# Second expert product turned round: w2 stationary, outputs as [d, token], and expert 0 on blocks of 512 tokens

## The chip, the cores and the metric

The kernel runs on one core of one Trainium2 chip. The metric is device time in microseconds of one execution, the median over the runs shown. TensorE does the matrix products (its matmul rows are called PE in the profile and its weight loads PEld), VectorE is DVE, ScalarE is ACT, GpSimd is POOL, and SyncE (SP) issues transfers.

## The reference, cut to what matters

Three parts follow each other. A delta-rule recurrence over 768 tokens of 4 batches and 8 heads gives x of 3072 x 384. A mixture of 8 experts, all of them on all tokens, is gated by P, which eight Sinkhorn iterations make from the logits of all tokens. A second network follows.

```
for t in range(768):                                   # per batch and head, 48 x 48 state
    y[t]  = q[t] @ state
    state = state + beta[t] * outer(k_n[t], v[t] - k_n[t] @ state)
x = y as [3072, 384]
P = sinkhorn(exp(x @ w_gate))                          # [3072, 8], 8 iterations over all tokens
for e in range(8):
    out += P[:, e:e+1] * (maximum(x @ w1[e], 0) @ w2[e])   # 384 -> 1024 -> 384
h = out @ w_in                                         # 384 -> 2048
result = (h * cos(h)) @ w_out                          # 2048 -> 384
```

## The kernel before, in words

**Products.** Every fp32 product is three TensorE passes over a head and a tail of each operand: head by head, head by tail, tail by head. `h_mms` (L112) makes 128 hidden columns f of a first product for a block of tokens: 9 matmuls (3 slices of d, 3 passes), w1 stationary, the tokens moving. `relu_split` (L134) takes them out of the PSUM bank: ACT writes the head, DVE the tail. `y_mms` (L125) makes the second product of 128 tokens: 3 matmuls with h stationary and 384 columns of w2 moving, so the result is [token, d]. In TensorE's rows L119 is a first product and L129 a second one.

**Attention.** The recurrence runs in 24 units of 128 tokens (chunks of 32 tokens of the 4 batches). `SEQ` (L29) spells, letter by letter, what TensorE does in a tick (one unit's time): K and k are the products of state with keys and queries (L311, L324), U, S and P the in-chunk solve, the state update and the output (L348, L362, L379), X the transposes of x (L397), G and g the gate's logits (L417, L431), T and B the transposes and the Gram products of a unit to come (L231, L249), N the operations of its normalisation on DVE and ACT (L191), W a weight split (L104), w filler matmuls (L558). Each m is half a step of expert 0 (`half`, L643): either one first product (`moe0_h`, L488) or one second product (`moe0_y`, L496). Between the letters `inv_some` (L547) issues operations of a triangular inversion on POOL (`inv_ops`, L275, rows L291 and L297); it must be done at every fourth tick, ahead of K. Until the first m, `fill` (L164) puts filler matmuls between the pieces of small matmuls.

```
29  SEQ = (..., "KXmNWmUmTGmkSmmNPgBmm", "KWmkmUXmTgBmSmPmTBNmm", "KmXkUTmNmSmmGPmmgBm")
638 mq.append((2 * ((s + 1) // FT) + 2, lambda s=s: moe0_h(s + 1)))
```

**Expert 0 before** goes over blocks of 256 tokens, as soon as two units are done (L635 to L639): eight m a tick from tick 2 on. A first product is 9 matmuls of 256 columns into one of two banks `hb`; a second product is 6 matmuls of 384 columns into `yb[0:2]`. Its output is written, not yet gated, to DRAM (`ysc`). What is left of expert 0 after the last tick runs at L715, with a Sinkhorn piece (`sk_some`, L481) at every fourth half; the remaining pieces run one a step in expert 1 (L921). `load_kq` and the weight loads of expert 0 go by SP's queue.

**Experts 1 to 7** are 336 steps of 512 tokens and 128 hidden columns (L777; 7 experts, 6 blocks, 8 slices f). A step of TensorE is `moe_h` of the next step (9 matmuls of 512 columns) and `moe_y` of this one (12 matmuls of 384 columns into the four banks `ybk`). After a block's eighth step DVE adds the four banks, each times its gate, to `acc` (L797; the gate is one scalar for each partition, a partition being a token). Weights come in groups of two slices f: `w_load` (L94) loads them into staging tiles by POOL's queue, `w_split` (L104) writes head and tail.

**The second network** wants its input as [d, token], so `x2_T` (L806) transposes `acc` on TensorE, three transposes for 128 tokens, and ACT and DVE split them. `net_step` and `net_y` (L873) work in three banks `hb2` (L827) and four `ybk`; the cosine's chain runs on ACT, POOL and DVE.

Of the kernel before, what the change touches and what calls it, by code (L numbers as in the profile page):

```python
# [34 lines left out]
def kernel(  # L35
# [28 lines left out]
    stg = ctx.enter_context(tc.tile_pool(name="stg", bufs=1))  # L64
# [7 lines left out]
    ysc = [dram.tile([128, 4, DM], F32, name=f"ysc{b}") for b in range(NB)]  # L72
# [6 lines left out]
    beta_sb = const.tile([128, S // C, C], F32, name="beta_sb")  # L79
# [11 lines left out]
    NG = FT // 2  # L91
    w1_t, w2_t, st1_t, st2_t = {}, {}, {}, {}

    def w_load(n):  # L94
        st1 = stg.tile([128, KD, 256], F32, tag="st1", name="st1")
        st2 = stg.tile([128, 2, DM], F32, tag="st2", name="st2")
        e, g = divmod(n, NG)
        a, b = w1[e, :, g * 256:(g + 1) * 256], w2[e, g * 256:(g + 1) * 256, :]
        q_ = nc.sync if n < NG else nc.gpsimd
        q_.dma_start(out=st1, in_=a.rearrange("(k p) f -> p k f", p=128))  # L100
        q_.dma_start(out=st2, in_=b.rearrange("(j p) d -> p j d", p=128))
        st1_t[n], st2_t[n] = st1, st2
# [30 lines left out]

    def relu_split(h, ps, nn):  # L134
# [861 lines left out]
```

## Time and profile before

| what | us |
|---|---|
| median of 3 runs | 2340.44 |
| lowest and highest run | 2336.85, 2342.12 |
| span of the profiled execution | 2340.3 |
| PE busy in it | 2266.8 (97%) |
| DVE busy | 1040.9 (44%) |
| ACT busy | 641.3 (27%) |
| POOL busy | 345.9 (15%) |

The span is the time of the one execution that the profiler recorded, from its first to its last instruction, and it stands beside the median within 0.2 us. Busy shares are means over stages that differ: the attention units end near 487 us, the rest of expert 0 near 510, experts 1 to 7 near 1926, and the second network fills the rest. "Granted clock" is TensorE's clock as a share of its full speed.

### The profile page before, as it was taken

To read this page: it belongs to the slowest core of one execution; us is meant where nothing else is said; L and a number is where in the kernel's file an instruction comes from. 1 tells how busy PE (TensorE), PEld (TensorE's weight loads), DVE (VectorE), ACT (ScalarE), POOL (GpSimd) and SP (SyncE) were. 2 spreads that over 40 slices of the span, in tenths; PEclk is the share of its full clock that TensorE was granted. 3 is DMA by queue.
4 is the path that set the end of the run, shared out by engine and by line. 5 is a ranking of instruction groups with operands and counts; after the bars stand their busy time and mean duration, and the time that the engine had idled before them with its cause. 6 is when DMAs were issued, how large, how long until landed. Compare 5 with 4: busy or idle time off the path is not lost.

```text
span 2340.3 us, 46677 instructions
## 1 busy us (share of the span) xinstructions
PE 2266.8 (97%) x20327; PEld 2027.2 (87%) x20327; DVE 1040.9 (44%) x2109; ACT 641.3 (27%) x1169; POOL 345.9 (15%) x599
## 2 busy tenths in 40 slices
PE   5889999999999999999999999999999999999998
PEld 3578888889999999999999999999999989888897
DVE  8455554345244324333333433433332226666665
ACT  1222222232122112112111211211111126566665
POOL 6256654210000000000000100000000011111111
PEclk7799999999999999999999999999999999999999
DMA  4233222153012002101100200110010130000000
GB/s 76 72 87 72 67 68 58 54 204 142 14 48 62 17 24 68 41 17 55 51 28 18 78 28 28 58 38 28 7 55 28 54 108 1 14 14 14 14 14 14
DMA packets 132221, 113.23 MB, mean 48 GB/s; under 512 B 80880, under 2 KB 121008, under 8 KB 131248
## 3 DMA queue, kind: packets, MB, share of 16 engines
q1 hardware_dynamic: 121936, 64.63, 10.2%
q0 software_dynamic: 10080, 45.62, 5.8%
q8 instruction: 159, 2.61, 0.4%
q14 instruction: 46, 0.38, 0.1%
HBM read 78.75 MB, written 31.46 MB: 47 GB/s over the span
## 4 chain that ended last, share of the span: by engine, by line
PE 89%; DVE 4%; POOL 4%; issue 2%; ACT 1%; DMA 1%; SPq 1%; POOLq 0%; ACTq 0%; DVEq 0%
PE hb L119 39%; PE yb L129 22%; PE pa L129 19%; PE pa L119 3%; POOL Xsys L297 1%; PE pa L341 1%; POOL tmp L291 1%; PE pa L354 1%; PE pa L385 1%; PE yb L167 1%; PE pa L238 1%; DVE Bst L304 1%; PE pa L257 0%; DVE S L374 0%; SPq L177 0%
## 5 line engine op out<-in xcount | busy, mean ns | idle before, releaser
L119 PE MATMUL hb<-x,w1t 128*128 128x512 f32 x3366 | 840.1, 394 | 0.0
L119 PEld LDWEIGHTS hb<-x,w1t 128*128 128x128 f32 x3366 | 624.9, 188 | 113.6
L136 DVE SCALAR_TENSOR_TENSOR h<-hb,h 128x512 fp32r<-128x512 f32 (+1 forms) x432 | 273.1, 632 | 964.2 <-ACT h L135 964.0
L129 PE MATMUL yb<-w2t,h 128*128 128x384 f32 x2952 | 605.6, 340 | 3.4 <-ACT tp L846 1.8
L135 ACT ACTIVATE h<-hb 128x512 fp32r<-128x512 f32 (+1 forms) x432 | 238.1, 551 | 1293.1 <-PE hb L119 1289.2
L129 PEld LDWEIGHTS yb<-w2t,h 128*128 128x128 f32 x2952 | 524.5, 188 | 42.1 <-ACT acc L882 3.1
L129 PE MATMUL pa<-w2t,h 128*128 128x384 f32 x2376 | 475.6, 334 | 0.0
L129 PEld LDWEIGHTS pa<-w2t,h 128*128 128x128 f32 x2376 | 420.7, 188 | 0.1
L100 POOL DMA_DIRECT2D st<-in_moe_w_dram x28 | 21.5, 769 | 1221.2 <-DVE w1t L109 1221.2
L119 PE MATMUL hb<-xb,w1t 128*128 128x256 f32 x864 | 130.0, 296 | 5.8 <-DVE xb L407 4.3
L119 PEld LDWEIGHTS hb<-xb,w1t 128*128 128x128 f32 x864 | 112.3, 194 | 11.3 <-DVE xb L407 4.7
L847 POOL TENSOR_SCALAR tp<-tp 128x512 f32<-128x512 f32 x96 | 60.1, 626 | 332.6 <-ACT tp L846 332.5
L297 POOL TENSOR_TENSOR Xsys<-Xsys,tmp 128x30 f32<-128x30 f32 (+9 forms) x150 | 80.5, 536 | 11.8
L866 ACT ACTIVATE h<-tp 128x512 fp32r<-128x512 f32 x96 | 60.7, 632 | 74.2 <-DVE tp L861 69.2
L855 ACT ACTIVATE tp<-tp 128x512 f32<-128x512 f32 x96 | 60.7, 632 | 68.1 <-DVE tp L852 68.1
L861 DVE TENSOR_TENSOR tp<-tp,hb 128x512 f32<-128x512 f32 x61 | 41.9, 688 | 80.1 <-ACT tp L860 80.1
L291 POOL TENSOR_TENSOR tmp<-Nsys,Xsys 128x30 f32<-128x30 f32 (+9 forms) x150 | 75.6, 504 | 11.2
L860 ACT ACTIVATE tp<-tp,small 128x512 f32<-128x512 f32 x96 | 68.7, 715 | 0.0
L871 DVE TENSOR_TENSOR h<-tp,h 128x512 fp32r<-128x512 f32 x96 | 65.6, 683 | 0.8 <-ACT h L866 0.8
L341 PEld LDWEIGHTS pa<-S,KT 48*32 48x32 f32 x2944 | 33.2, 107 | 21.8 <-DVE D L321 8.7
L119 PE MATMUL hb<-x 128*128 128x512 f32 x207 | 51.7, 394 | 0.0
L341 PE MATMUL pa<-S,KT 48*32 48x48 f32 x2944 | 42.8, 215 | 8.8 <-DVE D L321 6.3
(168 smaller groups left out, 1790.3 us busy)
## 6 DMA issues: line engine op xcount, KB each, us to landing
st<-in_moe_w_dram POOLq DMA_DIRECT2D x56, 384.0 KB, 4.0
xsc<-xb SPq DMA_DIRECT2D x24, 384.0 KB, 3.2
x<-xsc POOLq DMA_DIRECT2D x6, 1536.0 KB, 9.9
tp<-in_moe_w_in_dram SPq DMA_DIRECT2D x16, 384.0 KB, 3.5
wsa<-tp SPq DMA_DIRECT2D x32, 192.0 KB, 2.0
tp<-in_moe_w_out_dram SPq DMA_DIRECT2D x16, 384.0 KB, 3.3
wsb<-tp SPq DMA_DIRECT2D x32, 192.0 KB, 1.9
kr<-in_k_dram SPq DMA_DIRECT2D x96, 48.0 KB, 2.3
```

Source lines behind the costliest of these rows:

```text
L119: nc.tensor.matmul(out=ps[:, :nn], lhsT=w[:, a, kk, fs], rhs=x[:, b, kk, c0:c0 + nn], start=(i == 0), stop=(i == 3 * KD - 1),)
L129: nc.tensor.matmul(out=ps[:, :DM], lhsT=h[:, a, ts], rhs=w[:, b, f % 2, :], start=(first and i == 0), stop=(last and i == 2),)
L135: nc.scalar.activation(out=h[:, 0, :nn], in_=ps[:, :nn], func=ACTF.Relu)
L136: nc.vector.scalar_tensor_tensor(out=h[:, 1, :nn], in0=ps[:, :nn], scalar=0.0, in1=h[:, 0, :nn].bitcast(F32), op0=ALU.max, op1=ALU.subtract,)
L291: e.tensor_tensor(out=a, in0=Nsys[:, j + 1:, j:j + 1].to_broadcast([128, n, c1 - c0]), in1=Xsys[:, j:j + 1, c0:c1].to_broadcast([128, n, c ...
L297: e.tensor_tensor(out=x, in0=x, in1=a, op=ALU.subtract)
L341: nc.tensor.matmul(out=pa[i][b * C:(b + 1) * C, kq * 192 + j * D:kq * 192 + (j + 1) * D], lhsT=kt[r0:r0 + D, kq, j, b * C:(b + 1) * C], rh ...
L847: nc.gpsimd.tensor_scalar(out=a, in0=a, scalar1=-MAGIC, scalar2=1.0, op0=ALU.add, op1=ALU.mult)
L855: nc.scalar.activation(out=rr[i % 2], in_=rr[i % 2], func=ACTF.Abs)
L860: nc.scalar.activation(out=c, in_=rr[i % 2], func=ACTF.Sin, scale=-1.0, bias=half_pi)
L866: nc.scalar.activation(out=h[:, 0], in_=c, func=ACTF.Copy)
L871: nc.vector.tensor_tensor(out=h[:, 1], in0=cc[i % 2], in1=h[:, 0].bitcast(F32), op=ALU.subtract)
```

## The change

What it does:

- `yT_mms` takes the place of `y_mms` in all experts: w2 is the stationary side and h the moving one, 9 matmuls of 512 columns into three banks, one for each 128 rows of d; the result is [d, token].
- Expert 0 goes over blocks of 512 tokens with four units done ahead, four m a tick from tick 4 on instead of eight from tick 2; a first product has the one bank `hb`, a second one three banks `yb`. The gate's logits are made for 512 tokens at once, every fourth tick.
- Experts 1 to 7 alternate by block between the banks `pa[0:3]` and `yb`, and by step between `hb` and `pa[3]` once the Sinkhorn pieces are done.
- The gate now varies along the free axis: `sk_T` transposes P and writes it to DRAM; `p_load` loads a block's gate row, broadcast over the partitions, by SP's queue; `moe_acc` multiplies on DVE out of PSUM and adds on POOL, one of three slices at each of the steps f = 1, 2, 3 of the next block.
- `x2_split` (copy on ACT, subtraction on POOL) takes the place of `x2_T`; there are no transposes ahead of the second network. `hb2` has four banks throughout.
- One staging tile in place of two, all weight loads by SP's queue, and splits at other places. The inversion's identity constant is dropped, and its tiles and some others share the memory of weight tiles.

```diff
-SEQ = ("UwSNTWwBNP", "KkXUTSBNwPTBwW", "KXmNWmUmTGmkSmmNPgBmm", "KWmkmUXmTgBmSmPmTBNmm", "KmXkUTmNmSmmGPmmgBm")
+SEQ = ("UwSNTWwBNP", "KkXUTSBNwPTBwW", "KXNWUTkSNPB", "KWkUXTBSPTBN", "KXkUTmNSmGPBmgm")
...
-    hb = [psum.tile([128, 512], F32, name=f"hb{i}") for i in range(2)]
-    yb = [psum.tile([128, 512], F32, name=f"yb{i}") for i in range(2)]
+    hb = psum.tile([128, 512], F32, name="hb")
+    yb = [psum.tile([128, 512], F32, name=f"yb{i}") for i in range(KD)]
...
     def w_load(n):
-        st1 = stg.tile([128, KD, 256], F32, tag="st1", name="st1")
-        st2 = stg.tile([128, 2, DM], F32, tag="st2", name="st2")
+        st1, st2 = stage[-1][:, 0:768], stage[-1][:, 768:1536]
...
-        q_ = nc.sync if n < NG else nc.gpsimd
-        q_.dma_start(out=st1, in_=a.rearrange("(k p) f -> p k f", p=128))
+        nc.sync.dma_start(out=st1.rearrange("p (k f) -> p k f", k=KD), in_=a.rearrange("(k p) f -> p k f", p=128))
...
+    def yT_mms(banks, n, f, h, first, last):
+
+        w = w2_t[n]
+        for b, parts in ((0, (0, 1)), (1, (0,))):
+            for kd in range(KD):
+                for a in parts:
+                    nc.tensor.matmul(
+                        out=banks[kd], lhsT=w[:, a, f % 2, kd * 128:(kd + 1) * 128], rhs=h[:, b, :],
+                        start=(first and b == 0 and a == 0), stop=(last and b == 1),
+                    )
...
-        ops.append(lambda: eng.tensor_tensor(out=Xsys, in0=eye, in1=Nsys, op=ALU.subtract))
+        def first():
+
+            eng.tensor_scalar(out=Xsys, in0=Nsys, scalar1=-1.0, scalar2=None, op0=ALU.mult)
+            eng.memset(Xsys.rearrange("p t i -> p (t i)")[:, 0:C * C:C + 1], 1.0)
+
+        ops.append(first)
...
+    def sk_T():
+
+        flat = P.rearrange("p u e -> p (u e)")
+        nc.tensor.transpose(pa[3][:, 0:128], flat[:, 0:128], ident)
+        nc.tensor.transpose(pa[3][0:64, 128:256], flat[:, 128:192], ident)
...
+        nc.sync.dma_start(out=rows[0:128, :], in_=ptsb[:, 0:128])
...
     def moe0_h(s):
         m, f = divmod(s, FT)
-        ps = hb[s % 2]
-        h_mms(ps, f // 2, f, xb[m], 0, 256)
+        h_mms(hb, f // 2, f, xb[m], 0, 512)
...
-        for t in range(2):
-            y_mms(yb[t], f // 2, f, h, t, f == 0, f == FT - 1)
+        yT_mms(yb, f // 2, f, h, f == 0, f == FT - 1)
...
-        mq = [(2, lambda: moe0_h(0))]
+        mq = [(4, lambda: moe0_h(0))]
...
-                mq.append((2 * ((s + 1) // FT) + 2, lambda s=s: moe0_h(s + 1)))
+                mq.append((4 * ((s + 1) // FT) + 4, lambda s=s: moe0_h(s + 1)))
...
-                if len(mq) in (18, 11, 5):
+                if len(mq) in (10, 8, 5):
...
-            if i % 4 == 0:
+            if i % 2 == 0:
                 sk_some()
...
+        ysets = (pa[0:3], yb)
+
         def moe_h(i):
             e, b, f = steps[i]
-            h_mms(hb[i % 2], NG * e + f // 2, f, xblk[b], 0, 512)
+            hbk[i] = pa[3] if not sk and i % 2 == 0 else hb
+            h_mms(hbk[i], NG * e + f // 2, f, xblk[b], 0, 512)
...
-            for t in range(4):
-                y_mms(ybk[t], NG * e + f // 2, f, h, t, f == 0, f == FT - 1)
...
+            yT_mms(ysets[(i // FT) % 2], NG * e + f // 2, f, h, f == 0, f == FT - 1)
...
+        def p_load(e, b):
+
+            t = scr[0][:, (len(pb) % 2) * 512:(len(pb) % 2) * 512 + 512]
+            nc.sync.dma_start(
+                out=t.rearrange("p (t c) -> p t c", t=4),
+                in_=pts[4 * b:4 * b + 4, e, :].partition_broadcast(128),
+            )
+            pb[e, b] = t
+
+        def moe_acc(n, kd):
...
+            t = scr[0][:, 1024:1536]
+            nc.vector.tensor_tensor(out=t, in0=ysets[n % 2][kd], in1=pb[e, b], op=ALU.mult)
+            nc.gpsimd.tensor_tensor(out=acc[b][:, kd, :], in0=acc[b][:, kd, :], in1=t, op=ALU.add)
...
-        def x2_T(b, t):
-            for kk in range(KD):
-                nc.tensor.transpose(pa[3][:, kk * 128:(kk + 1) * 128], acc[b][:, t, kk * 128:(kk + 1) * 128], ident)
...
+        def x2_split(b, kd):
+            nc.scalar.activation(out=x2[b][:, 0, kd, :], in_=acc[b][:, kd, :], func=ACTF.Copy)
+            nc.gpsimd.tensor_tensor(
+                out=x2[b][:, 1, kd, :], in0=acc[b][:, kd, :], in1=x2[b][:, 0, kd, :].bitcast(F32), op=ALU.subtract
+            )
...
+            if n and 1 <= f <= 3:
+                moe_acc(n - 1, f - 1)
...
         w2_load(7)
+        for kd in (0, 2, 1):
+            moe_acc(len(steps) // FT - 1, kd)
...
-            if f in (2, 5, 8, 11) and b + 1 < NB:
+            if f in (2, 5, 8) and b + 1 < NB:
...
-                x2_T(b + 1, t)
+                x2_split(b + 1, kd)
```

## Rows read from the trace of the kernel before

**Rows 1.** The page's picture of the span in 40 equal slices of 58.5 us, of which the line of TensorE's busy share and the line of its granted clock, both in tenths.

```profile
PE   5889999999999999999999999999999999999998
PEclk7799999999999999999999999999999999999999
```

**Rows 2.** Busy time by stretch. The columns are the stretch (us from the span's start), its length, the busy time with the count of instructions of PE, PEld, DVE, ACT and POOL, then the granted clock, the share of the DMA engines and GB/s. The stretches are tick 1; the ticks 8 to 15; the ticks 16 to 23; tick 24 with the rest of expert 0; experts 1 to 7; and, last, 3.4 us of tick 10.

```profile
76.87:103.78 26.91, 26.39 (x537) 14.66 (x536) 6.91 (x26) 5.99 (x13) 2.27 (x3) 0.71 0.20 36
225.16:367.52 142.36, 131.65 (x3681) 116.15 (x3680) 76.79 (x212) 39.60 (x104) 76.92 (x138) 0.99 0.27 64
367.52:487.50 119.98, 117.80 (x3183) 105.84 (x3183) 43.16 (x105) 32.18 (x83) 32.66 (x61) 1.00 0.19 53
487.50:509.83 22.33, 20.56 (x141) 19.39 (x140) 9.79 (x18) 9.29 (x20) 5.66 (x8) 1.00 0.72 248
509.83:1926.20 1416.37, 1416.37 (x7114) 1282.82 (x7113) 508.72 (x919) 260.89 (x424) 47.77 (x70) 1.00 0.15 49
...
273.30:276.70 3.40, 3.40 (x74) 2.82 (x72) 0.55 (x1) 0.37 (x1) 3.01 (x6) 0.50 0.24 84
```

**Rows 3.** The chain of work that ended last, in order of time, near the end of the experts: start in us, duration, engine, the tile written and the line, and the number of instructions. L119 is nine matmuls of 512 columns, L129 six of 384. From one start to the next is what the nine or six take.

```profile
1905.52 2.08 PE hb L119 x9
1907.61 1.06 PE yb L129 x6
1908.67 1.04 PE pa L129 x6
1909.71 2.08 PE hb L119 x9
1911.79 2.04 PE pa L119 x9
1913.83 1.06 PE yb L129 x6
```

**Rows 4.** TensorE's timeline in the rest of expert 0: start, duration with the tail of the last matmul, line, tiles, shapes (stationary side, then moving side) and count.

```profile
502.16 1.23 PE L119 MATMUL hb<-xb,w1t 128*128 128x256 f32 x9
503.23 1.21 PE L129 MATMUL yb<-w2t,h 128*128 128x384 f32 x6
504.27 1.23 PE L119 MATMUL hb<-xb,w1t 128*128 128x256 f32 x9
```

**Rows 5.** TensorE's timeline in the second network, around one group of transposes (L808).

```profile
2007.52 0.49 PE L808 MATMUL pa<-ident,acc 128*128 128x128 f32 x3
2007.77 2.30 PE L119 MATMUL pa<-x 128*128 128x512 f32 x9
2009.90 0.33 PE L129 MATMUL yb<-x,h 128*128 128x384 f32 x1
```

**Rows 6.** TensorE's timeline from tick 2 to tick 4: the first two of four groups of K in tick 2 (filler matmuls lie between the groups), K of tick 4 with the idle time before it and what ended that, and the first half-step of expert 0 in tick 4.

```profile
103.78 0.32 PE L341 MATMUL pa<-S,KT 48*32 48x48 f32 x16
104.35 0.32 PE L341 MATMUL pa<-S,KT 48*32 48x48 f32 x16
...
155.31 1.26 PE L341 MATMUL pa<-S,KT 48*32 48x48 f32 x64 [3.36 <-DVE D L321]
159.56 1.80 PE L119 MATMUL hb<-xb,w1t 128*128 128x256 f32 x9
```

**Rows 7.** POOL's timeline: the last operation of the inversion ahead of tick 4.

```profile
148.25 0.25 POOL L297 TENSOR_TENSOR Xsys<-Xsys,tmp 128x30 f32<-128x30 f32 x1
```

**Rows 8.** The timeline of all engines in tick 14: T's first four transposes, a second product of expert 0, the first reduction of a normalisation, the state's adds, and the gate with the idle time before it.

```profile
335.98 0.66 PE L238 MATMUL pa<-ident,kr 128*128 128x128 f32 x4
...
337.98 1.21 PE L129 MATMUL yb<-w2t,h 128*128 128x384 f32 x6
...
339.07 0.55 DVE L215 TENSOR_REDUCE nrm<-sq 128x8 f32<-128x384 f32 x1
...
343.27 1.13 DVE L374 TENSOR_TENSOR S<-S,pa 128x192 f32<-128x192 f32 x4
344.45 0.29 PE L421 MATMUL pa<-xb,wg 128*16 128x256 f32 x1 [0.65 <-DVE S L374]
```

**Rows 9.** TensorE's timeline in tick 19: its K, one first product of expert 0 between small matmuls, and K of the next tick.

```profile
414.34 0.81 PE L341 MATMUL pa<-S,KT 48*32 48x48 f32 x64
...
418.27 1.34 PE L119 MATMUL hb<-xb,w1t 128*128 128x256 f32 x9
...
427.86 0.81 PE L341 MATMUL pa<-S,KT 48*32 48x48 f32 x64
```

**Rows 10.** TensorE's timeline in tick 10: the gate's first matmul, with the idle time before it.

```profile
272.83 0.29 PE L421 MATMUL pa<-xb,wg 128*16 128x256 f32 x1 [2.30 <-DVE S L374]
```

**Rows 11.** Groups of instructions by line and shape: line, engine, operation, tiles, shapes, count | busy us, mean ns of one | idle time of the engine before them and what ended it.

```profile
L136 DVE SCALAR_TENSOR_TENSOR h<-hb,h 128x512 fp32r<-128x512 f32 x336 | 232.6, 692 | 869.5 <-ACT h L135 869.5
L135 ACT ACTIVATE h<-hb 128x512 fp32r<-128x512 f32 x336 | 201.3, 599 | 1125.5 <-PE hb L119 1121.7 <-DVE small L464 3.8
L201 POOL TENSOR_TENSOR kb<-kr,beta_sb 128x384 f32<-128x384 f32 x24 | 20.6, 858 | 65.7 <-DVE kr L224 38.7 <-PE hb L119 22.2 <-DVE tmp L291 3.1
```

**Rows 12.** The timeline of all engines where the experts end and the second network begins: the last two gated adds, and the first weight loads behind them with their idle time.

```profile
1927.44 1.14 DVE L797 SCALAR_TENSOR_TENSOR acc<-yb,P,acc 128x384 f32<-128x384 f32 x2
1928.12 1.00 PEld L129 LDWEIGHTS yb<-w2t,h 128*128 128x128 f32 x6 [2.16 <-ACT tp L846]
```

**Rows 13.** Transfers by issue: tiles, queue, kind and count, KB of one, median us from issue to landing.

```profile
st<-in_moe_w_dram POOLq DMA_DIRECT2D x56, 384.0 KB, 4.0
```

More of the change, by code (lines that the diff above doesn't have):

```diff
@@ L425, in pe_gate @@
             nc.tensor.matmul(
-                out=pa[3][0:E, 0:256], lhsT=wg[:, kk, 0, :], rhs=x[:, 1, kk, :], start=False, stop=(kk == KD - 1),
+                out=pa[3][0:E, :], lhsT=wg[:, kk, 0, :], rhs=x[:, 1, kk, :], start=False, stop=(kk == KD - 1),
             )
-        lt[m] = ap1.tile([2 * E, 256], F32, tag="lt", name="lt")
-        nc.scalar.activation(out=lt[m], in_=pa[3][0:2 * E, 0:256], func=ACTF.Copy)
+        nc.scalar.activation(out=ltm, in_=pa[3][0:2 * E, :], func=ACTF.Copy)
     def pe_gate2(m):
-        t = lt.pop(m)
-        for i in range(2):
+        for i in range(4):
             nc.tensor.matmul(
-                out=pa[3][:, 384 + i * E:384 + (i + 1) * E], lhsT=t[:, i * 128:(i + 1) * 128], rhs=two,
-                start=True, stop=True,
+                out=pa[3][:, i * E:(i + 1) * E], lhsT=ltm[:, i * 128:(i + 1) * 128], rhs=two, start=True, stop=True,
             )
         nc.scalar.activation(
-            out=logits[:, 2 * m:2 * m + 2, :], in_=pa[3][:, 384:384 + 2 * E].rearrange("p (i e) -> p i e", i=2), func=ACTF.Copy
+            out=logits[:, 4 * m:4 * m + 4, :], in_=pa[3][:, 0:4 * E].rearrange("p (i e) -> p i e", i=4), func=ACTF.Copy
         )
@@ L477, in sk_cols @@
             sk_rows()
-    sk.extend([sk_max, sk_max_t, sk_exp] + [lambda i=i: sk_cols(i) for i in range(8)])
+    def sk_T():
+        flat = P.rearrange("p u e -> p (u e)")
+        nc.tensor.transpose(pa[3][:, 0:128], flat[:, 0:128], ident)
+        nc.tensor.transpose(pa[3][0:64, 128:256], flat[:, 128:192], ident)
+        nc.vector.tensor_copy(out=ptsb[:, 0:128], in_=pa[3][:, 0:128])
+        nc.scalar.activation(out=ptsb[0:64, 128:256], in_=pa[3][0:64, 128:256], func=ACTF.Copy)
+        rows = pts.rearrange("u e p -> (u e) p")
+        nc.sync.dma_start(out=rows[0:128, :], in_=ptsb[:, 0:128])
+        nc.sync.dma_start(out=rows[128:192, :], in_=ptsb[0:64, 128:256])
+    sk.extend([sk_max, sk_max_t, sk_exp] + [lambda i=i: sk_cols(i) for i in range(8)] + [sk_T])
     def sk_some():
@@ L498, in moe0_y @@
         h = h0_t.pop(s)
-        for t in range(2):
-            y_mms(yb[t], f // 2, f, h, t, f == 0, f == FT - 1)
+        yT_mms(yb, f // 2, f, h, f == 0, f == FT - 1)
         if f == FT - 1:
-            for t in range(2):
-                u = 2 * m + t
-                y = hp.tile([128, DM], F32, tag="y0", name="y0")
-                nc.scalar.activation(out=y, in_=yb[t][:, :DM], func=ACTF.Copy)
-                nc.sync.dma_start(out=ysc[u // 4][:, u % 4, :], in_=y)
-    NS0 = (NU // 2) * FT
+            for kd in range(KD):
+                if m in acc:
+                    nc.scalar.activation(out=acc[m][:, kd, :], in_=yb[kd], func=ACTF.Copy)
+                else:
+                    y = ap2.tile([128, 512], F32, tag="y0", name="y0")
+                    nc.scalar.activation(out=y, in_=yb[kd], func=ACTF.Copy)
+                    nc.sync.dma_start(out=ysc[m][:, kd, :], in_=y)
+    NS0 = NB * FT
     with tc.manual_schedule():
@@ L619, in load_block @@
             nc.gpsimd.dma_start(out=xblk[b], in_=xsc[b])
-            nc.sync.dma_start(out=acc[b], in_=ysc[b])
+            if b < NB - 1:
+                nc.sync.dma_start(out=acc[b], in_=ysc[b])
         def begin_blocks():
@@ L717 @@
             i += 1
-            if i % 4 == 0:
+            if i % 2 == 0:
                 sk_some()
-        ybk = [yb[0], yb[1], pa[0], pa[1]]
         cv = []
-        tp = [hp.tile([128, 3 * 512], F32, tag="xb", name=f"tp{i}") for i in range(2)]
+        tpt = hp.tile([128, 2, 3 * 512], F32, tag="xb", name="tp")
+        tp = [tpt[:, i] for i in range(2)]
         craw = tp[0][:, 0:768].bitcast(I32).rearrange("p (a b w) -> p a b w", a=3, w=2)
@@ L923 @@
                 xq.pop(0)()
-            if i == 1:
+            n = i // FT
+            if n and 1 <= f <= 3:
+                moe_acc(n - 1, f - 1)
+            if i == FT:
+                assert not sk
+                p_load(0, 0)
+            if i >= FT and f == 0:
+                p_load(*((e, b - 1) if b else (e - 1, NB - 1)))
+            if e == 1 and f == 4 and b:
+                p_load(0, b)
+            if e == E - 1 and b == NB - 1 and f == 4:
+                p_load(e, b)
+            if i == 0:
                 w_split(NG + 3)
@@ L933 @@
                     w_load(n + 1)
-                if last and f in (1, 3, 5):
-                    g = (f + 1) // 2
-                    w_split(n + g)
-                    if g < 3:
-                        w_load(n + g + 1)
+                if last and f in (2, 4, 6):
+                    w_split(n + f // 2)
+                    if f < 6:
+                        w_load(n + f // 2 + 1)
                 if i >= 2 * FT and i % 8 not in (1, 2):
@@ L948 @@
                     w2_load(b - 1)
-                if 1 <= b <= 4 and f == 4:
-                    x2_T(0, b - 1)
+                if 2 <= b <= 4 and f == 4:
+                    x2_split(0, b - 2)
                 if last and f == 0:
```

136 lines of the change are left out of this document (66 added, 70 removed).

## The prediction, made before the changed kernel ran

> **What bounds the kernel now.** I read the page's shares first, then the stages, then single lines. TensorE is busy nearly throughout and its granted clock is full from the eighth of the 40 slices on [rows 1], so the question is how many TensorE microseconds the change removes and where TensorE waits. The stage table [rows 2] splits the run: from 509.8 to 1926.2 us (experts 1 to 7, 336 steps) no idle time is shown; in the units (ticks 8 to 15, then 16 to 23) TensorE is idle 10.7 and 2.2 us. The stage ahead of 104 us is latency-bound at a clock of 0.71. What is saved in a step of the experts therefore comes off the end 336 times, and what is done in the units has to be priced tick by tick.
>
> What a matmul costs there: nine of 512 columns after the six-and-six of 384 take 2.08 us, twelve of 384 take 2.10, and where nine of 512 follow nine of 512 the second nine take 2.04 [rows 3]. Nine of 256 take 1.07 and six of 384 take 1.04 [rows 4]. Settled, that is 0.119, 0.173 and 0.227 us each: 0.053 to 0.054 per 128 columns and 0.013 fixed. Beside the fixed part, a run of matmuls of a new width starts slower: 0.04 us over nine, 0.03 over twelve.
>
> **Gain 1, experts 1 to 7.** The second product had 12 matmuls of 384 columns a step and gets 9 of 512: the same 4608 columns, three fixed parts fewer (0.04 us), and no change of width within the stage (0.07 us). Settled, 18 x 0.2267 = 4.08 us against 4.19 [rows 3]: 0.106 us x 336 = 35.6 us less. Not shown before is how w2 as stationary side and h as moving side behave; the bounds are both nines as slow as a first nine (4.16, gain 8 us) and both settled (36 us). A loss is excluded, since columns stay and instructions fall. I take the settled end: the row nearest to 512 after 512 is the second nine of [rows 3].
>
> **Gain 2, no transposes ahead of the second network.** Three transposes take 0.25 us and the nine after them 2.13 instead of 2.08 [rows 5]: 24 x 0.30 = 7.2 us less, all on TensorE. In its place ACT copies and POOL subtracts; both run beside TensorE, two steps ahead of the use, so I cost them at nothing. If POOL's subtract (some 1.1 us, from 0.86 for 384 elements [rows 11]) delayed the cosine chain behind it, TensorE would wait at the second product; 15 places, under 1 us each.
>
> **The units, stage by stage.** Expert 0 starts once four units are done instead of two, in halves twice as long, four a tick instead of eight.
>
> *Ticks 2 and 3, to the first half-step in tick 4.* Before, 103.78 to 159.56 us [rows 6], 15 small halves done within. They leave, so 15 x 1.06 = 16 us of TensorE work moves behind. The time doesn't shrink by it: without "m" the filler matmuls stay on until tick 4, and a piece of 64 small matmuls then takes 2.3 us (four groups of 0.57 [rows 6]) where it took 0.75. Walking the dependences with such pieces (U behind the weight split of the same tick, S behind U's copy, state adds, P, B and its evictions, the next K) I get 26 us for tick 2, 25.6 for tick 3 and 11 from K to the first half-step of tick 4 (normalisation and inverse transpose on DVE ahead of D): 62.7 against 55.8, +7. Tick 1, which has no expert in it either, took 26.9 [rows 2]. Bounds: if only POOL's inversion, ending at 148.3 [rows 7], counted, -5; two ticks like tick 1 at a low clock, +13.
>
> *Ticks 4 to 7.* The pieces and four big halves come to 65.5 us by the same pieces as below; before, it was 65.6 from that first half-step at 159.56 [rows 6] to 225.16, where the next stage begins [rows 2]. Nothing.
>
> *Ticks 8 to 15.* A late tick before: 13.5 us [rows 9], of which eight halves are 8.4, four entries and exits between small and large matmuls 0.2 each, the attention pieces 4.35. New: pieces 4.35, four halves 8.16, three entries 0.6, a quarter of the gate's 2.1, and a new wait: K is followed by the short X and then k, which writes the banks that D still reads; D ends about 0.85 us after K, X covers 0.4, so 0.45 a tick. With T and B (some 0.8 each; T's four, the first row of [rows 8], are 0.66 without their tail) and 0.4 of odd stalls that is 16.1. Then the normalisation: it stands on DVE behind the half-step's subtract and ahead of the state adds, and P (or the gate) waits for the adds. In tick 14 the half-step ends at 337.98, normalisation starts at 339.07, adds end at 344.40, and the gate still waited 0.65 us with 4.4 us of matmuls in between [rows 8]. New, relu and subtract of 512 columns (0.60 and 0.69 [rows 11]) delay it by 0.5, and between half-step and P stand only S and one big half, 2.95 us: a wait of 3 us (2.2 where POOL is idle, 4.2 where it is busy). 19.05 x 8 = 152.4 against 142.4 [rows 2]: +10 (4 to 20).
>
> *Ticks 16 to 23*, without normalisation: 14.3 x 8, and one T, = 115.5 against 120.0 [rows 2]: -4.5.
>
> *Tick 24 and the rest of expert 0.* Before 22.3 us [rows 2]. New: tick 24 has four halves, X and the gate, 11.8; then 13 halves are left, 26.6; Sinkhorn's small products 1.2; some 3 of waits, as each weight load now starts when the one staging tile is free, lands 4.0 us later [rows 13], and two of the three splits come two and three halves after the last. That is 42.6, and 1.5 where two first products share the one bank: +21.8 (19 to 26). Here the work moved out of ticks 2 and 3 is paid.
>
> Sum of the units: 7 + 0 + 10 - 4.5 + 21.8 = +34.3 us.
>
> **The join to the second network.** TensorE waited for DVE's last adds until 1928.12 [rows 12], two adds taking 1.14. Now three multiplies of 0.69 on DVE alternate with three POOL adds through one scratch tile, about 4.7 us instead of 2.3; the two free banks come first, so I take +2 (0 to 3). Sinkhorn products that leave the expert stage: -1.
>
> **At nothing:** gating adds in the experts (DVE 509 of 1416 us busy, POOL 48 [rows 2]; two sets of banks give them a block's time); the gate rows' loads and weight loads now on SP, asked for a step or more ahead; if such a load came late, DVE would stand at the multiply with the next subtract behind it, and TensorE would wait after 2 us. The dropped identity constant and the cheaper first step of an inversion lie beside other work.
>
> **Sum:** +34.3 - 35.6 - 7.2 + 2 - 1 = -7.5. The profiled execution took 2340.3 us and the median of the runs is 2340.4, so its sum needs no shift: 2333 us. A measurement of this kernel can tell about 0.2%, 4.7 us, from no change.
>
> **Rivals.**
> *The second product doesn't settle (slower).* The price of the experts' step falls short: 4.12, as the run of eighteen in [rows 3], gives 22 us and 2347; 4.16 gives 8 us and 2360. Against it, the second nine at 2.04 repeats no reading of other data; for it, no row has the roles swapped. It decides once the step is over 4.11. The Trainium skill, "TensorE: Matmul & The Clock Gate", section "Back-to-back issue gap", has a warm gap of columns/2.4 plus 2.5 ns; by that, three matmuls fewer are worth 7.5 ns a step, 2.5 us in all, and the sum would be 2366. The rows here have 13 ns where it has 2.5, so they disagree. Chance 0.16.
>
> *The clock falls in the new waits (slower).* In tick 10 TensorE waited 2.30 us for the same adds, and the next 3.4 us ran at a granted 0.50, the lower level of 1.2 GHz [rows 2, 10], losing 1.7 us. Eight waits of 3 us in ticks 8 to 15 could each bring that: 14 us at 1.7, 27 if it lasts twice as long; 2347 to 2360. It decides from about seven such falls; with two to six, 2336 to 2343, no change. The Trainium skill's same page (part 1, the clock gate) says that an idle array falls back to 1.2 GHz; tick 10 agrees. Slower 0.18, no change 0.18.
>
> *The front costs less (faster).* If POOL's inversion alone bounds ticks 2 and 3 and D's wait is covered, the units cost +18 instead of +34: 2308 to 2322. For it, [rows 7]; against it, tick 1 had no inversion and was as long. Chance 0.10.
>
> **Numbers.** The sum as it stands, 2322 to 2336, has 0.38; with the cheaper front, faster has 0.48; no change 0.18; slower 0.16 + 0.18 = 0.34. The likeliest case's own range is 2322 to 2336. The range that leaves out no more than 2 in 10 reaches from the cheap front to the unsettled step: 2308 to 2360.
>
> **What would show it.** Right: steps of 4.08 us in the experts with 18 matmuls at 0.227; no transposes in the second network; first half-step of expert 0 near 166 us; waits of about 3 us for the state adds in ticks 8 to 15 and 0.45 ahead of k; the experts' stage starting near 544. Wrong: steps over 4.11 us; a granted clock of 0.5 in more than a few ticks; half-steps already near 155 us; or TensorE idle within the experts, behind a late load or split.

## The result: 21 us slower, and the profile after

The median is 2361.67 us (2358.13 to 2369.20, 4 runs) against 2340.56 us before on the same chip (the three runs of the table above and a fourth): a ratio of 1.0101, 95% interval [1.0076, 1.0125]. The forecast was 2333 with a range to 2360. The direction was wrong, and the time lies just outside the range.

The profiled execution has a span of 2358.1 us, 17.8 more than before. First the page's two lines that answer to [rows 1], in 40 slices:

```profile
PE   5889889996999999999999999999999999999998
PEclk7879999998999999999999999999999999999999
```

One slice stands out behind the start: the tenth, from 531 us on, with TensorE busy for six tenths. Next the stages, with the columns of [rows 2]: tick 1; from tick 2 to the first half-step of expert 0; on to tick 8; ticks 8 to 15; 16 to 23; tick 24 with the rest of expert 0; experts 1 to 7; the second network.

```profile
75.61:96.91 21.30, 20.60 (x536) 12.27 (x536) 8.43 (x32) 6.14 (x14) 2.28 (x3) 1.00 0.30 62
96.91:165.30 68.39, 59.20 (x1192) 31.48 (x1192) 30.08 (x70) 11.54 (x26) 41.26 (x69) 0.72 0.31 76
165.30:228.87 63.57, 58.90 (x1529) 45.33 (x1527) 35.11 (x95) 14.59 (x34) 39.05 (x70) 0.98 0.25 50
228.87:385.44 156.57, 133.74 (x3477) 103.42 (x3477) 73.81 (x197) 36.32 (x82) 77.11 (x139) 0.96 0.24 58
385.44:503.88 118.44, 115.44 (x2974) 88.83 (x2973) 39.79 (x88) 27.16 (x59) 33.16 (x62) 1.00 0.19 53
503.88:562.69 58.81, 41.68 (x181) 32.57 (x179) 20.40 (x48) 14.23 (x23) 3.29 (x6) 0.85 0.71 268
562.69:1942.01 1379.32, 1376.92 (x6080) 1140.17 (x6079) 495.63 (x843) 243.94 (x397) 196.23 (x149) 1.00 0.18 51
1942.01:2351.08 409.07, 402.99 (x1999) 359.01 (x1997) 255.62 (x397) 243.17 (x408) 85.11 (x119) 1.00 0.05 14
```

Set beside the stages before, cut at the same points (the network from its first product of the regular steps, 1924.15 us before and 1942.01 after), this is the account; what lies behind the network is 0.5 us shorter:

| stage | before | after | difference | forecast |
|---|---|---|---|---|
| to the start of tick 2 | 103.78 | 96.91 | -6.9 | 0 |
| tick 2 to the first half-step in tick 4 | 55.78 | 68.39 | +12.6 | +7 |
| on to tick 8 | 65.60 | 63.57 | -2.0 | 0 |
| ticks 8 to 15 | 142.36 | 156.57 | +14.2 | +10 |
| ticks 16 to 23 | 119.98 | 118.44 | -1.5 | -4.5 |
| tick 24, rest of expert 0 | 22.33 | 58.81 | +36.5 | +21.8 |
| experts 1 to 7 | 1414.32 | 1379.32 | -35.0 | -36.6 |
| join and second network | 408.67 | 409.07 | +0.4 | -5.2 |
| sum | | | +18.3 | -7.5 |

**Experts.** The steps are what was forecast. Near the end of the stage the chain of waits, in the columns of [rows 3], has nines of 2.04 us and nothing else (L123 is a first product, L144 a second one):

```profile
1925.85 2.04 PE yb L144 x9
1927.89 4.08 PE pa L123 x18
1931.97 2.04 PE yb L144 x9
```

**The rest of expert 0.** Here stands the largest miss. The timeline of all engines (start, duration, engine and line, tiles, and the idle time before with what ended it):

```profile
515.81 3.30 POOL L640 DMA_DIRECT2D x<-xsc  x6 [76.06 <-DMA ysc<-y]
...
525.03 0.37 SPq L104 DMA_DIRECT2D scr<-in_moe_w_dram  x1
525.89 0.37 SPq L105 DMA_DIRECT2D scr<-in_moe_w_dram  x1
...
541.00 0.84 ACT L112 ACTIVATE w1t<-scr 128x768 fp32r<-128x768 f32 x1 [13.49 <-DMA scr<-in_moe_w_dram]
541.87 0.96 DVE L113 TENSOR_TENSOR w1t<-scr,w1t 128x768 fp32r<-128x768 f32 x1 [13.64 <-ACT w1t L112]
545.41 0.84 ACT L112 ACTIVATE w2t<-scr 128x768 fp32r<-128x768 f32 x1 [3.57 <-DMA scr<-in_moe_w_dram]
546.28 0.96 DVE L113 TENSOR_TENSOR w2t<-scr,w2t 128x768 fp32r<-128x768 f32 x1 [3.45 <-ACT w2t L112]
547.16 0.15 DVE L472 TENSOR_SCALAR small<-pa 128x1 f32<-128x1 f32 x1
549.93 0.59 PE L484 MATMUL pa<-small,ones 128*128 128x8 f32 x2 [16.37 <-DVE small L481]
```

Read it from the bottom. TensorE waits 16.37 us for a Sinkhorn sum. On DVE that sum (behind L472) stands in order behind the weight split (L113), the split waits for ACT's half (L112), and that waits for loads: the one asked for at 525.03 lands at 541.0, after 16 us, and the one for w2, asked for at 525.89, lands at 545.4, after 19.5 us, where the forecast had 4.0 from [rows 13]. Six to nine microseconds ahead of them POOL had asked for all six token blocks at once, 1536 KB each. Before, POOL's queue held the weight loads too:

```profile
498.76 0.77 POOL L100 DMA_DIRECT2D st<-in_moe_w_dram  x1 [8.10 <-DVE w1t L109]
500.56 0.58 POOL L630 DMA_DIRECT2D x<-xsc  x1 [0.21 <-issue]
...
508.60 0.57 POOL L619 DMA_DIRECT2D x<-xsc  x1
525.11 0.77 POOL L100 DMA_DIRECT2D st<-in_moe_w_dram  x1 [15.93 <-DVE w1t L109]
526.70 1.12 POOL L619 DMA_DIRECT2D x<-xsc  x2
```

A weight load there waits for its staging tile (15.93 us), and the two block loads behind it wait with it. The change took the weight loads out of that queue, and nothing held the blocks back.

**Ticks 8 to 15.** In tick 8 the state's adds (L392) stand on DVE behind the normalisation, which begins with L228, and the gate's product (L437) waits for them:

```profile
236.41 0.54 DVE L228 TENSOR_REDUCE nrm<-sq 128x8 f32<-128x384 f32 x1
...
239.20 1.14 DVE L392 TENSOR_TENSOR S<-S,pa 128x192 f32<-128x192 f32 x4
...
240.39 0.41 PE L437 MATMUL pa<-xb,wg 128*16 128x512 f32 x1 [2.26 <-DVE S L392]
```

TensorE's timeline in tick 9: the output product waits for the state's adds (L392), and the first product behind it takes 3.58 us from start to start (263.59 to 267.17) where one at full clock takes 2.2.

```profile
261.87 0.88 PE L403 MATMUL pa<-U,Pp 32*32 32x48 f32 x64 [2.61 <-DVE S L392]
...
263.59 3.74 PE L123 MATMUL hb<-xb,w1t 128*128 128x512 f32 x9
267.17 1.08 PE L144 MATMUL yb<-h,w2t 128*128 128x512 f32 x4
```

And the four such stretches in the columns of [rows 2]; the granted clock is the value behind POOL's:

```profile
263.59:267.17 3.58, 3.58 (x13) 2.85 (x10) 0.89 (x4) 0.00 (x0) 3.19 (x6) 0.57 0.03 7
301.52:304.92 3.40, 3.40 (x14) 2.71 (x10) 0.89 (x4) 0.00 (x0) 0.62 (x1) 0.61 0.00 0
342.08:345.67 3.59, 3.59 (x13) 2.85 (x10) 0.89 (x4) 0.00 (x0) 3.20 (x6) 0.57 0.00 0
362.47:366.10 3.63, 3.63 (x13) 2.87 (x11) 0.88 (x4) 0.00 (x0) 2.92 (x10) 0.56 0.02 5
```

The comparisons leave out disturbed executions; runs 7 and 9 below had one each (2493 and 4545 us), whose cause is not known, and the times given for these two are the medians of their other three.

### The profile page after: what moved, and what is told of

It reads as the page before. It is cut to its first block, busy times and chain, and to the rows that moved or that the text cites. A ratio compares the mean times of both kernels' runs of the same rounds, so it can differ in the third digit from the quotient of the medians.

```text
span 2358.1 us, 43469 instructions
## 1 busy us (share of the span) xinstructions
PE 2254.9 (96%) x18757; PEld 1845.9 (78%) x18757; DVE 1016.1 (43%) x1997; ACT 612.6 (26%) x1074; POOL 513.1 (22%) x696
## 3 DMA queue, kind: packets, MB, share of 16 engines
q1 hardware_dynamic: 164880, 97.76, 15.5%
## 4 chain that ended last, share of the span: by engine, by line
PE 89%; DVE 5%; issue 2%; DMA 1%; ACT 1%; POOL 1%; SPq 0%; DVEq 0%; POOLq 0%; ACTq 0%
PE hb L123 21%; PE pa L123 18%; PE yb L144 17%; PE pa L144 14%; PE pa L133 4%; PE yb L133 4%; PE yb L123 2%; PE pa L359 2%; PE yb L180 1%; PE pa L372 1%; PE pa L403 1%; DMA scr<-in_moe_w_dram 1%; PE pa L270 1%; PE pa L251 1%; DVE S L392 1%
## 5 line engine op out<-in xcount | busy, mean ns | idle before, releaser
L144 PE MATMUL yb<-h,w2t 128*128 128x512 f32 x1944 | 479.9, 391 | 0.0
L123 PE MATMUL pa<-x,w1t 128*128 128x512 f32 x1800 | 441.7, 390 | 0.0
L144 PEld LDWEIGHTS yb<-h,w2t 128*128 128x128 f32 x1944 | 362.7, 188 | 76.0
L123 PE MATMUL hb<-x,w1t 128*128 128x512 f32 x1656 | 406.5, 390 | 2.4 <-DVE h L151 2.4
L123 PEld LDWEIGHTS pa<-x,w1t 128*128 128x128 f32 x1800 | 337.4, 188 | 68.5
L144 PE MATMUL pa<-h,w2t 128*128 128x512 f32 x1512 | 370.0, 389 | 0.0
L123 PEld LDWEIGHTS hb<-x,w1t 128*128 128x128 f32 x1656 | 310.2, 188 | 66.4 <-DVE h L151 2.9
L144 PEld LDWEIGHTS pa<-h,w2t 128*128 128x128 f32 x1512 | 283.9, 188 | 58.9
L123 PE MATMUL hb<-xb,w1t 128*128 128x512 f32 x432 | 119.9, 424 | 1.9 <-DVE h L151 0.7
L123 PEld LDWEIGHTS hb<-xb,w1t 128*128 128x128 f32 x432 | 83.6, 202 | 22.2 <-issue 1.6
L133 PE MATMUL pa<-w2t,h 128*128 128x384 f32 x360 | 75.6, 342 | 3.6 <-DVE h L909 2.0
L133 PEld LDWEIGHTS pa<-w2t,h 128*128 128x128 f32 x360 | 63.9, 188 | 12.7 <-DVE h L909 4.2
```

The lines of the kernel that those rows point to most:

```text
L123: nc.tensor.matmul(out=ps[:, :nn], lhsT=w[:, a, kk, fs], rhs=x[:, b, kk, c0:c0 + nn], start=(i == 0), stop=(i == 3 * KD - 1),)
L133: nc.tensor.matmul(out=ps[:, :DM], lhsT=h[:, a, ts], rhs=w[:, b, f % 2, :], start=(first and i == 0), stop=(last and i == 2),)
L144: nc.tensor.matmul(out=banks[kd], lhsT=w[:, a, f % 2, kd * 128:(kd + 1) * 128], rhs=h[:, b, :], start=(first and b == 0 and a == 0), stop= ...
```

## The experiments

All but the eighth start from the changed kernel. "Stage" times are those of their profiled executions, cut as in the table above; a ratio is to the kernel before on the same chip. "Less" is a difference of medians; the changed kernel's 2361.67 us was taken beside a kernel before of 2340.56 us, runs 1 to 4 beside one of 2338.46 us, so by the ratios runs 1 to 4 gain 1 to 2.5 us more than the medians say.

**1. Block loads held back.** A tiny copy on POOL, which needs the next step's hidden tile, goes ahead of each of the loads of blocks 1 to 5.

```diff
             if xq and i % 2 == 0:
+                nc.gpsimd.tensor_copy(out=small[:, 3, 4:5], in_=h_t[i + 1][:, 1, 0:1].bitcast(F32))
                 xq.pop(0)()
```

> The changed kernel, with one tiny POOL copy ahead of each load of a token block for blocks 1 to 5; the copy reads the hidden tile of the step, so POOL asks for these blocks one by one in expert 1 instead of all at once at 516 us. Theory A (the second weight load of expert 1 took 16 us because 9.4 MB of block loads had been asked for just ahead of it): the load lands about 4 to 7 us after its issue, the wait of 16.4 us ahead of the column sums of Sinkhorn falls under 4 us and the time falls by 12 to 16 us, to 2346 to 2350. Rival B (one staging tile: the load can only start when the split before it is done, and the two splits lie two halves apart): the wait stays over 8 us, the time falls by less than 8. Rival C (the Sinkhorn operations themselves): no change.

Measured: 2349.28 us, ratio 1.0041 [1.0022, 1.0061], 12.4 us less than the changed kernel. Tick 24 and the rest of expert 0 take 43.3 us instead of 58.8:

```profile
505.61:548.92 43.31, 40.60 (x180) 31.38 (x179) 20.44 (x48) 14.36 (x23) 0.63 (x1) 1.00 0.53 183
```

The load that took 16 us now lands 3.2 us after it was asked for (526.78 to 530.01), and TensorE's wait is 0.80 us:

```profile
517.52 0.63 POOL L640 DMA_DIRECT2D x<-xsc  x1 [76.49 <-DMA ysc<-y]
...
526.78 0.37 SPq L104 DMA_DIRECT2D scr<-in_moe_w_dram  x1
530.01 0.84 ACT L112 ACTIVATE w1t<-scr 128x768 fp32r<-128x768 f32 x1 [0.75 <-DMA scr<-in_moe_w_dram]
...
536.11 0.39 PE L484 MATMUL pa<-small,ones 128*128 128x8 f32 x2 [0.80 <-DVE small L481]
```

Theory A holds. The one staging tile (rival B) is still there, and so are Sinkhorn's operations (C).

**2. Weight loads back on POOL's queue.**

```diff
-        nc.sync.dma_start(out=st1.rearrange("p (k f) -> p k f", k=KD), in_=a.rearrange("(k p) f -> p k f", p=128))
-        nc.sync.dma_start(out=st2.rearrange("p (j d) -> p j d", j=2), in_=b.rearrange("(j p) d -> p j d", p=128))
+        q_ = nc.sync if n < NG else nc.gpsimd
+        q_.dma_start(out=st1.rearrange("p (k f) -> p k f", k=KD), in_=a.rearrange("(k p) f -> p k f", p=128))
+        q_.dma_start(out=st2.rearrange("p (j d) -> p j d", j=2), in_=b.rearrange("(j p) d -> p j d", p=128))
```

> The changed kernel, with the weight loads of experts 1 to 7 back on POOL's queue, as before the change; one staging tile stays. Theory A (on POOL's queue a weight load that waits for its staging tile holds the block loads behind it back, and moving it to SP let all six go at once): the wait of 16.4 us goes to under 4 us and the time falls by 10 to 16 us, less if POOL's gated adds now stand behind a waiting load. Rival B (one staging tile): the wait stays over 8 us. If the queue has nothing to do with it, no change from 2361.7.

Measured: 2355.96 us, ratio 1.0066 [1.0047, 1.0084], 5.7 us less, under the 10 to 16 expected. The stage itself went from 58.8 to 45.4 us, as the theory has it, and its longest wait for the sums is 1.86 us. Up to tick 24 the program is the changed kernel's, yet this profiled execution was 11.5 us later there (515.39 against 503.88): tick 1 had a lower clock (26.8 us at 0.72) and ticks 8 to 15 took 160.4 us. So the queue move is the cause of the stage's length. The median of eight runs stays short of the stage's 13.4 us; that the stages ahead vary between executions may be the reason, and is not shown.

**3. Normalisation behind the state update.**

```diff
-SEQ = ("UwSNTWwBNP", "KkXUTSBNwPTBwW", "KXNWUTkSNPB", "KWkUXTBSPTBN", "KXkUTmNSmGPBmgm")
+SEQ = ("UwSNTWwBNP", "KkXUTSBNwPTBwW", "KXNWUTkSNPB", "KWkUXTBSPTBN", "KXkUTmSNmGPBmgm")
```

> The changed kernel, with the normalisation of a unit to come issued after the state update S instead of ahead of it, in every tick from 4 on. Theory (in ticks 8 to 15 the output product or the gate waits 2.0 to 2.9 us for the state's adds, which stand on DVE behind the normalisation): the eight waits, 19 us in all, go, and with them the four stretches at a lower granted clock behind them (1.2 to 1.4 us each); ticks 8 to 15 fall from 156.6 to 133 to 140 us and the time by 16 to 24 us, to 2338 to 2346. Rival (the normalisation is merely late elsewhere: T of the next tick, or the tail of the hidden tile, waits for it): the time falls by less than 8 us.

Measured: 2335.78 us, ratio 0.9983 [0.9964, 1.0002], 25.9 us less, a little more than expected. Ticks 8 to 15 take 136.3 us instead of 156.6:

```profile
232.19:368.50 136.31, 129.74 (x3477) 101.40 (x3476) 73.59 (x197) 35.85 (x82) 77.36 (x140) 0.97 0.29 67
```

In tick 9 the adds now come ahead of the normalisation's reduction, and the wait ahead of the output product is 0.36 us, on the weight side, in place of 2.61:

```profile
263.70 1.14 DVE L392 TENSOR_TENSOR S<-S,pa 128x192 f32<-128x192 f32 x4
264.75 0.55 DVE L228 TENSOR_REDUCE nrm<-sq 128x8 f32<-128x384 f32 x1
265.41 0.75 PEld L403 LDWEIGHTS pa<-U,Pp 32*32 32x32 f32 x64 [0.36 <-DVE nrm L228]
265.41 0.88 PE L403 MATMUL pa<-U,Pp 32*32 32x48 f32 x64
```

The eight waits are gone, and the rival falls as to size. One new wait came, in tick 8: TensorE waits 1.99 us for ACT's copy of the gate's logits (L444), and the second product behind it takes 4.1 us in place of 2.2. That is why the stage's granted clock is 0.97 and not 1.00.

```profile
249.31 1.66 PE L448 MATMUL pa<-two,w2t 16*128 16x8 f32 x8 [1.99 <-ACT w2t L444]
```

**4. No fillers in ticks 2 to 4.**

```diff
         def tick(tau, seq):
+            filling[0] = filling[0] and tau < 2
```

> The changed kernel, without the filler matmuls between the pieces of ticks 2, 3 and 4 (ticks 0 and 1 keep them). Theory (the fillers make a piece of 64 small matmuls 2.3 us or more long and so set the time to the first half-step of expert 0): from the start of tick 2 to that half-step 55 to 60 us instead of 68.4, the time falls by 8 to 13 us. Rival (the chains of DVE, ACT and POOL set it, and a lower granted clock takes what the fillers gave): within 4 us of 68.4, or longer, and more of the stretch at a granted 0.5.

Measured: 2353.48 us, ratio 1.0062 [1.0040, 1.0085], 8.2 us less. From tick 2 to the first half-step it is 52.7 us instead of 68.4, at a granted clock of 0.59 instead of 0.72; ticks 8 to 15 gave 7 us back at 0.92:

```profile
94.19:146.92 52.73, 28.98 (x1066) 24.10 (x1066) 30.54 (x71) 11.54 (x26) 41.35 (x69) 0.59 0.40 97
209.75:373.33 163.58, 139.38 (x3477) 108.37 (x3476) 74.89 (x197) 36.31 (x82) 76.68 (x139) 0.92 0.24 56
```

The fillers set the length of that stretch. Without them the clock is lower, and in this stretch that costs less than they do.

**5. Both edits, 1 and 3**, as shown there.

> The changed kernel with both edits: block loads 1 to 5 asked for one by one in expert 1, and the normalisation issued after the state update. Theory (two separate causes in two stages, the flood of block loads in the rest of expert 0 and the late state adds in ticks 8 to 15): the savings add up, 15.5 us from the end of tick 23 to expert 1 (43 us there) and 20 us in ticks 8 to 15 (136 us there), 2320 to 2330, faster than before by 0.4 to 0.9%. Rival (one of them is given back, because an earlier stage end meets the same transfers): 2335 to 2345.

Measured: 2321.41 us, ratio 0.9933 [0.9913, 0.9953]. Ticks 8 to 15 take 133.8 us and the rest of expert 0 43.4: the two savings add up.

**6. Edits 1, 3 and 4**, as shown there.

> The run with both edits, and without the filler matmuls in ticks 2, 3 and 4. Theory (without fillers those ticks are 15.7 us shorter, as in the run that left them out alone; the 7 us which that run lost again in ticks 8 to 15 were stretches at a lower clock behind the waits for the state's adds, which are gone here): 12 to 17 us less than with both edits alone, 2305 to 2316, ticks 8 to 15 at 133 to 138 us. Rival (the clock falls later whatever the waits): 6 to 9 us less, with ticks 8 to 15 over 141.

Measured: 2302.63 us, ratio 0.9845 [0.9829, 0.9862], 18.8 us less than with two edits, a little more than expected. Ticks 8 to 15 take 136.4 us, so most of the 7 us of run 4 were falls of the clock behind the waits for the adds: there it fell behind six of the eight. A fall is left in tick 8, behind the wait for ACT's copy (2.00 us) that run 3 has too.

**7. Join and split, on top of 6.** Three scratch tiles at the join, the subtraction of `x2_split` on DVE.

```diff
-            t = scr[0][:, 1024:1536]
+            t = scr[0][:, 1024 + 512 * j:1536 + 512 * j]
...
-            moe_acc(len(steps) // FT - 1, kd)
+            moe_acc(len(steps) // FT - 1, kd, kd)
...
-            nc.gpsimd.tensor_tensor(
+            nc.vector.tensor_tensor(
```

> The run with three edits, and in addition three scratch tiles in place of one for the last block's gating at the join, and the subtraction of the second network's input split on DVE in place of POOL. Theory (at the join three multiplies alternate with three POOL adds of 1.3 us through one tile, which cost the network's first two second products 5.5 us; in the network POOL's 1.3 us subtraction stands ahead of the cosine chain's rounding and costs 0.22 us at 13 of 15 places): join shorter by 2 to 3.5 us, network shorter by 2 to 3 us, 4 to 6 us in all. Rival (DVE, with the subtraction, is itself late for the hidden tile's tail): the 0.22 us stay, or grow, and only the join's part comes.

Measured: 2300.22 us, ratio 0.9846 [0.9824, 0.9867]: no gain clear of noise against run 6 (0.9845). The network from its first product went from 409.1 to 406.3 us, and that came from the split alone. The join's first four steps took 22.5 us in both. The multiplies no longer wait, but POOL does its three adds in a row, and the cosine chain's rounding (L886) stands behind them. TensorE then waits 2.69 us for the hidden tile, and the next first product takes 3.39 us, at a granted 0.58, where one takes 2.1:

```profile
1887.51 1.88 DVE L843 TENSOR_TENSOR scr<-yb,scr 128x512 f32<-128x512 f32 x3
1888.34 3.80 POOL L844 TENSOR_TENSOR acc<-acc,scr 128x512 f32<-128x512 f32 x3 [3.20 <-DVE scr L843]
1892.11 0.62 POOL L886 TENSOR_SCALAR tp<-tp 128x512 f32<-128x512 f32 x1
1892.76 0.69 DVE L890 SCALAR_TENSOR_TENSOR tp<-tp,hb 128x512 f32<-128x512 f32 x1 [2.78 <-POOL tp L886]
```

The join's half of the theory fell. The rival, that DVE would be late with the subtraction, fell too, for the split's half came.

**8. The kernel before, with the normalisation behind the state update.**

```diff
-SEQ = ("UwSNTWwBNP", "KkXUTSBNwPTBwW", "KXmNWmUmTGmkSmmNPgBmm", "KWmkmUXmTgBmSmPmTBNmm", "KmXkUTmNmSmmGPmmgBm")
+SEQ = ("UwSNTWwBNP", "KkXUTSBNwPTBwW", "KXmNWmUmTGmkSmmNPgBmm", "KWmkmUXmTgBmSmPmTBNmm", "KmXkUTmmSNmmGPmmgBm")
```

> The kernel before the change, with the normalisation issued after the state update in every tick from 4 on, and the half-step that stood ahead of the update drawn together with the one behind it. Theory (the wait for the state's adds in ticks 8 to 15 came with the change: with eight short half-steps two stood between the normalisation and the output product and covered most of it): ticks 8 to 15 shorter by 2 to 8 us of 142.4, time 2331 to 2338, so much less than the 20 us that the same move gives the changed kernel. Rival (the wait was as large before): 15 us or more.

Measured: 2327.96 us, ratio 0.9956 [0.9937, 0.9974]. Ticks 8 to 15 take 133.6 us instead of 142.4 [rows 2]: 8.8 us, somewhat more than expected and less than half of what the same move gives the changed kernel. So the late adds cost the kernel before too, and the change made them dearer. The same execution shows that the time of tick 1 is not the change's doing: its tick 1 is the code of the kernel before, and it took 21.3 us at full clock, not 26.9 at 0.71.

```profile
78.11:99.41 21.30, 20.61 (x536) 12.28 (x535) 8.42 (x32) 6.14 (x14) 2.27 (x3) 1.00 0.30 62
218.80:352.41 133.61, 130.05 (x3682) 115.10 (x3681) 76.89 (x212) 39.72 (x104) 77.07 (x138) 1.00 0.29 69
```

**9. The join's adds later, on top of 7.**

```diff
+            def add():
+                nc.gpsimd.tensor_tensor(out=acc[b][:, kd, :], in0=acc[b][:, kd, :], in1=t, op=ALU.add)
+
+            late.append(add) if defer else add()
...
+            if late and i % 2:
+                late.pop(0)()
```

> The run with join and split edits, and with the last block's three POOL adds at the join issued only behind the second products of network steps 1, 3 and 5. Theory (with three scratch tiles the multiplies no longer wait, but three POOL adds, 3.8 us in a row, stood ahead of the cosine chain's rounding on POOL and gave the time back): the network's first four products take 17 to 19 us instead of 22.5, and the time falls by 3 to 5 us against the run with join and split edits. Rival (the adds cost the chain about 0.2 us at each of three places, and DVE's three multiplies ahead of the chain are the wait): under 2 us.

Measured: 2300.66 us, ratio 0.9847 [0.9827, 0.9867]. In the profile the first four steps take 18.0 us (22.5 in run 7) and the network 401.9 us (406.3): the theory's mechanism and size. In the time nothing of it shows (2300.22 us and 0.9846 in run 7), as the rival had it; a gain in the total is not shown.

**10. What one matmul costs beside its columns.** Each second-product matmul of experts 1 to 7 in two of 256 columns. The columns are all there, but the sums in the banks don't come out as the reference's, so only the time is read.

```diff
-                    nc.tensor.matmul(
-                        out=banks[kd], lhsT=w[:, a, f % 2, kd * 128:(kd + 1) * 128], rhs=h[:, b, :],
...
+                    for c in range(0, 512, cw):
+                        nc.tensor.matmul(
+                            out=banks[kd][:, c:c + cw], lhsT=w[:, a, f % 2, kd * 128:(kd + 1) * 128], rhs=h[:, b, c:c + cw],
...
-            yT_mms(ysets[(i // FT) % 2], NG * e + f // 2, f, h, f == 0, f == FT - 1)
+            yT_mms(ysets[(i // FT) % 2], NG * e + f // 2, f, h, f == 0, f == FT - 1, 256)
```

> The changed kernel, with each matmul of the second product of experts 1 to 7 cut into two of 256 columns: 18 of 256 columns in place of 9 of 512. Theory (a matmul has a fixed part of 0.013 us beside 0.053 us for 128 columns): nine fixed parts more a step, 0.12 us, and 0.04 to 0.07 us for the change of width, so steps of 4.23 to 4.27 us and a time 51 to 65 us longer. Rival (a fixed part of 0.0025 us): 0.02 us, and the change of width, so steps of 4.14 to 4.17 us and 21 to 31 us longer.

Measured, in a single execution: 2409.04 us, 47.4 us longer than the changed kernel. Experts 1 to 7 take 1426.0 us, 46.7 more, 0.139 a step:

```profile
1002.01 2.07 PE hb L123 x9
1004.08 2.15 PE pa L145 x18
1006.24 2.07 PE pa L123 x9
```

Nine more matmuls cost 2.15 - 2.04 = 0.11 us, 0.012 each, and the change of width 0.03 on the nine behind it. That is the theory's price for a matmul and a smaller cost of the change of width than its 0.04 to 0.07, so the time stays 4 us under the range expected.

## Why the prediction was wrong, point by point

- **Experts: right.** Steps of 4.08 us, and 35.0 us less where 35.6 and 1 were forecast. The choice of the settled end was good, and run 10 confirms the two prices behind it (0.013 fixed, a slower start after a change of width). The rival of an unsettled second product is out. The Trainium skill ("TensorE: Matmul & The Clock Gate", section "Back-to-back issue gap") has 2.5 ns beside the columns in the gap of a warm matmul by itself. That does not agree with run 10, where matmuls in a row have 12 ns; the measurement decides.
- **Tick 24 and the rest of expert 0: the step that failed.** It priced a weight load at the 4.0 us of [rows 13] and took "some 3" for waits; the two loads took 16 and 19.5 us and the wait was 16.4. It put the move of the weight loads to SP's queue at nothing because they are asked for a step ahead, and did not ask what a load that left POOL's queue had been holding back. With the blocks held back (run 1) the stage takes 43.3 us; the prediction's terms were 42.6 and 1.5. This step mended alone gives run 1's 2349 us, inside the range but still slower than before, so the direction hangs on the next points too.
- **Ticks 8 to 15: right in mechanism, short in size.** The adds stood behind the normalisation, as worked out; the eight waits were 2.00 to 2.87 us (3 forecast), 19.2 in all. The wait of 0.45 us a tick ahead of k did not come: there is one, of 0.32 us, in the eight ticks. The clock fell behind four of the eight waits, to 0.56 to 0.61 over the next first product (0.50, the level of 1.2 GHz, from 263.87 to 266.37 us in tick 9), which cost 1.2 to 1.4 us each, 5.4 in all. The rival wanted seven of eight to decide; here four came on top of the forecast. The Trainium skill's rule in part 1 of the same page ("TensorE: Matmul & The Clock Gate"), that an idle array falls back to 1.2 GHz, agrees with these four rows; four waits of like length had no such fall.
- **Ticks 2 to 4: at the upper bound.** +12.6 against +7, bound +13. The fillers were priced at full clock, a group of small matmuls with its filler at 0.57 us [rows 6]; the stretch ran at 0.72, and late in it such a group takes 0.88 us (157.53 to 158.41). Run 4 shows their price: 15.7 us.
- **Join and second network: the gain was lost again.** The transposes went; 20 of the 24 groups lay in this stage, 6.0 of the 7.2 us, and the other four in the experts. POOL's subtraction was not free (2.8 us, run 7), and the join cost 3.7 us where 2 was taken: its first four steps take 22.5 us, and 18.8 before without their one group of transposes. POOL's add takes 1.3 us, about twice DVE's multiply; run 7 shows that ending the alternation is not enough, and run 9 that the three adds ahead of the cosine chain are what the join waits for.
- **To tick 2: -6.9, chance.** 5.6 of it is tick 1's clock, which differs between executions of the same code (run 8). The 0.71 that the prediction gives for the whole stage ahead of 104 us is tick 1's; the whole had 0.77.

With the flood (15.5 us, run 1) and the falls of the clock (5.4 us) taken off, the profiled 2358.1 would be 2337: these two are most of the 25 us between forecast and result. Of what is left, the fillers (5.6 over the forecast), join and network (5.6) and ticks 16 to 23 (3, cause not known) are on one side, and the start (-6.9) and ticks 4 to 7 (-2) on the other.

The change is worth having once its companions are mended: run 9 takes 2300.7 us (0.9847 of before), and the old layout with the same normalisation move (run 8), the only mend tried on it, 2328.0 us (0.9956).

## What to carry to other kernels

When transfers move from one queue to another, ask what the queue that they leave will do sooner: a load that waited for its buffer was also the brake on everything behind it, and the freed loads land on the very transfer that is needed next. When work between two dependent steps gets coarser (four long half-steps for eight short ones), list for each waiting product what stands ahead of its input on the in-order engine, and issue the urgent operation first. A filler that keeps a clock up has to be priced at the clock that it really gets: here leaving it out won 15.7 us of its stretch at a lower clock, though 7 us of that were lost again until the waits behind it were gone.

## What the runs showed of the hardware

Six loads of 1536 KB asked for within 3.3 us made a load of 384 KB behind them, on another queue, take 16 us instead of 3.2 (run 1), and the next one 19.5 us. The granted clock of tick 1 came out at 0.71 or 1.00 in executions of the same code, 26.9 or 21.3 us. Waits of about 2.0 to 2.9 us were followed by the lower clock in four of eight cases.
